# Holding back the early conversions of the last weight: a set begin, spacing, and another place in the sync queue

## The chip, the cores and the metric

The kernel runs on one core of one Trainium2 chip. The metric is the device time of one execution in microseconds (us), lower is better; the median of three runs of the kernel before is 587.26 us. PE is the matrix engine, DVE the vector engine, ACT the scalar engine, POOL the GpSimd engine, SP the sync engine, on which almost every transfer is issued. Each of them takes its instructions strictly in the order in which the program lists them.

## What is computed

An attention over 2 batches, 8 heads, 768 positions and head size 64, in which each query sees a band of neighbours and 24 block summaries, and then two feed-forward blocks over the 1536 tokens that it gives:

```
scores = [band(q k^T), q (block max of k)^T + log 32];  a = softmax(scores);  x = a [v ; block mean of v]
h = ((x w1) * (x w2)) w3 w_out            # 512 -> 1024 -> 1024 -> 512
h2 = h w_in;  y = (h2 * clip(h2+3,0,6)/6) w_out2     # 512 -> 2048 -> 512
```

The weights arrive as 8-byte floats.

## The kernel before

Products are done in three passes over pairs of high and low parts, so every operand tile has two halves: `slot(s)[:, 0]` the rounded value, `slot(s)[:, 1]` the rest. **A conversion** of one 128x512 weight tile is a load of 512 KB into a buffer `raw` (SP), two ACT operations (`to_f32`: a scaled copy `c<-raw` of the upper word, and a shift of the lower word in place), two DVE operations on `c`, and then in `to_hi_lo` an ACT copy (high part) and a POOL subtraction (low part). The buffers `raw` and `c` are four each and are taken in turn (`take`).

The weight that is used last, `w_out2` (16 tiles), has no place on the chip yet while attention runs. `convert_out` converts each of its tiles ahead of time, puts high and low part back into the `raw` buffer they came from, and `spill` writes them out to a buffer `wo` in memory (512 KB, on SP); `fetch` brings them back later. So one `raw` buffer goes through load, conversion and write-out before the next load may use it.

The program is not written in the order in which it runs. Every step is an entry of a `Graph` (`g.op`) with its engine, an estimated length, a due time, and the buffers that it reads and writes. `schedule` walks a clock of its own through the entries: an entry is ready when those it depends on are done by the estimates, and of the ready entries of an engine the one that is due first is taken. What it leaves is one fixed order per engine; on the chip, semaphores hold each instruction until its data are there, and everything behind it on the same engine waits with it.

The stretch of the change lies between the loop over token blocks and the second feed-forward block. The loop (`ab`, `acc1`; three blocks `j` of eight pairs) gives PE 36 matmuls of 128x512 for a pair; between them stand the attention tiles of the next block: scores (`probabilities`), softmax on DVE, POOL and ACT, and in `attend` the transposes (PE), two copies `pt` out of the banks (ACT and DVE), the product with V (PE) and its write to `arena`. Each pair's result passes ACT as `ta` and `arena<-tg`. Behind the loop, `sums_of_x` and `w_in_group` prepare the operands of the second block; `w_in_group` uses the same `raw` and `c` buffers, in turn behind the sixteen of `convert_out`. The call stands ahead of both and gives all sixteen tiles the same due time:

```
        sums_of_x(due)
        for n in range(NFC2):
            convert_out(due, w2_in[NFC2 + tile_of(n)], ("wo", n))
        w_in_group(due, 0)
```

An entry with a far due time is still taken as soon as its engine has nothing more urgent that is ready.

Of the kernel before, what the change touches and what calls it, by code (L numbers as in the profile page):

```python
# [30 lines left out]
P = 128  # L31
# [18 lines left out]
NFC, NFC2 = DFF // P, DFF2 // P  # L50
# [10 lines left out]
class Graph:  # L61
# [10 lines left out]
        self.ops = []  # L72
        self.writer, self.readers = {}, {}

    def op(self, eng, ns, due, fn, reads=(), writes=(), lock=False):
        i = len(self.ops)
        deps = set()
        for k in reads:
            if k in self.writer:
                deps.add(self.writer[k])  # L80
            self.readers.setdefault(k, []).append(i)
        for k in writes:
            if k in self.writer:
                deps.add(self.writer[k])
            deps.update(self.readers.get(k, ()))
            self.writer[k] = i
            self.readers[k] = []
        deps.discard(i)
        self.ops.append((eng, ns, due, fn, deps, lock or eng == "pool"))
        return i  # L90

    def schedule(self):
        n = len(self.ops)
        left = [len(o[4]) for o in self.ops]
        users = [[] for _ in range(n)]
        for i, o in enumerate(self.ops):
            for d in o[4]:
                users[d].append(i)

        due = [o[2] if o[0] == "pe" else self.LAST for o in self.ops]  # L100
        for i in range(n - 1, -1, -1):
            for u in users[i]:
                e = self.ops[i][0]
                due[i] = min(due[i], due[u] - self.ops[i][1] - self.LAT.get(e, 40))
        ready_at = [0.0] * n
        engines = sorted({o[0] for o in self.ops})
        free = dict.fromkeys(engines, 0.0)
        coming = {e: [] for e in engines}
        ready = {e: [] for e in engines}
        for i, o in enumerate(self.ops):  # L110
            if not left[i]:
                heapq.heappush(coming[o[0]], (0.0, i))
        order = []
        port = 0.0
        while True:
            best = None
            for e in engines:
                while coming[e] and coming[e][0][0] <= free[e]:
                    i = heapq.heappop(coming[e])[1]
                    heapq.heappush(ready[e], (due[i], i))  # L120
                if ready[e]:
                    t = free[e]
                elif coming[e]:
                    t = coming[e][0][0]
                else:
                    continue
                if best is None or t < best[0]:
                    best = (t, e)
            if best is None:
                break  # L130
            t, e = best
            if not ready[e]:
                free[e] = t
                continue
            i = heapq.heappop(ready[e])[1]
            eng, ns = self.ops[i][:2]
            order.append((t, i))
            if self.ops[i][5]:
                t = max(t, port)
                port = t + ns  # L140
            free[e] = t + ns
            for u in users[i]:
                same = self.ops[u][0] == e
                at = t + ns + (0 if same and e == "pe" else 35 if same else self.LAT.get(e, 40))
                ready_at[u] = max(ready_at[u], at)
                left[u] -= 1
                if not left[u]:
                    heapq.heappush(coming[self.ops[u][0]], (ready_at[u], u))
        assert len(order) == n
        return sorted(order)  # L150
# [8 lines left out]
L3N = 1  # L159
DUE_FF = 29.0  # L160
AHEAD, BEHIND = -27.8, -143.7


def build(tc, qd, kw, vw, kt, vt, consts, wp_in, w12_in, w2_in, out):
# [68 lines left out]
        turn[name] += 1  # L233
        return t

    def load(due, out_fn, in_ap, nbytes, writes):
        g.op("sp", max(450, nbytes / 400.0), due, lambda: nc.sync.dma_start(out=out_fn(), in_=in_ap), (), writes)  # L237

    def to_f32(due, src, pieces=1, banks=None, n_raw=N_RAW):

        r, c = take("raw", n_raw), take("c", N_C)
        kr, kc = ("raw", r), ("c", c)
# [5 lines left out]
        for i in range(pieces):  # L248
            e = slice(i * ne, (i + 1) * ne)
            kri, kci = (kr, kc) if pieces == 1 else ((kr, i), (kc, i))  # L250
            ra = raws[r][:, e]
            load(due - 6 * us, lambda ra=ra: ra, src[:, e], P * ne * 8, [kri] + [kr] * (i == 0))
            w = ra.bitcast(U32).rearrange("p (n two) -> p n two", two=2)
            wf = ra.bitcast(F32).rearrange("p (n two) -> p n two", two=2)
            hw, lw = w[:, :, 1], w[:, :, 0]
# [50 lines left out]

    def spill(due, key, src_fn, reads):
        d = spilled[key]
        g.op("sp", 1300, due, lambda: nc.sync.dma_start(out=d, in_=src_fn()), reads, [key])

    def fetch(due, s, key):
        d = spilled[key]
        g.op("sp", 1300, due, lambda: nc.sync.dma_start(out=slot(s).bitcast(F32), in_=d), [key], both(s))

    def convert_out(due, src, key, lo="pool"):

        r, c, parts = to_f32(due, src)
        e, f, cf, keys = parts[0]
        w = raws[r].bitcast(F32R).rearrange("p (two n) -> p two n", two=2)
        kr = [("raw", r)]  # L320
        to_hi_lo(due, 1, lambda: cf, keys, lambda: w[:, 0, :], lambda: w[:, 1, :], kr, kr, lo)
        spill(due, key, lambda: raws[r].bitcast(F32).rearrange("p (two n) -> p two n", two=2), kr)
# [355 lines left out]
    with tc.manual_schedule():  # L678
# [169 lines left out]

        sums_of_x(due)
        for n in range(NFC2):  # L850
            convert_out(due, w2_in[NFC2 + tile_of(n)], ("wo", n))
        w_in_group(due, 0)
        w_in_group(due, 1)
        prev = []
# [168 lines left out]
```

## Time and profile before

| | before |
|---|---|
| median of 3 runs (lowest to highest) | 587.26 us (587.2 to 587.62) |
| the profiled execution, its own time | 587.12 us |
| its span in the trace | 585.1 us |
| PE busy, share of the span | 541.2 us, 92% |
| DVE, ACT, POOL busy | 345.5, 283.0, 217.5 us |
| mean granted clock of PE | 0.985 |

PE is busy for 92% of the span; the span is 2.02 us shorter than the execution's own time. Clock values are shares of PE's full clock (1.00 is 2.4 GHz, 0.5 is 1.2 GHz); a mean between them is a mixture of the two over a stretch.

### The profile page before, as it was taken

Reading aid. Unit: us, or ns where it says so; the run is one execution under the profiler, and the core shown is the slowest. Engines: PE = TensorE matmul, PEld = TensorE weight load, DVE = VectorE, ACT = ScalarE, POOL = GpSimd, SP = SyncE. Lnnn points to the kernel's source line nnn. Section 1 sums busy time; section 2 is a strip of 40 time slices with the busy share of each in tenths; the row PEclk is TensorE's granted clock in tenths of the full one; section 3 lists DMA queues with packets and bytes.
Section 4 is the critical chain, followed back from the end, with each engine's and each line's share of the span. In section 5 each row is a group of like instructions: output and inputs, shape, how many; then the busy total and the mean of one; then the engine's idle time right before and its main releaser. Section 6 shows DMA issues by size and latency. Waiting matters only on the chain.

```text
span 585.1 us, 8146 instructions
## 1 busy us (share of the span) xinstructions
PE 541.2 (92%) x3032; PEld 441.3 (75%) x3032; DVE 345.5 (59%) x464; ACT 283.0 (48%) x483; POOL 217.5 (37%) x178
## 2 busy tenths in 40 slices
PE   0679999999999939969999999999999999999997
PEld 0457788887778728758888888888888888888885
DVE  5899978877895737477853487888545222221000
ACT  2788877437445434434444487675544422222001
POOL 0578656894443324329134374555300000000000
PEclk9999999999999978979999999999999999999999
DMA  8999873756437664627354547733489921001521
GB/s 307 375 349 333 233 251 109 216 176 211 150 113 242 203 234 115 229 73 289 107 206 181 185 169 259 272 153 147 154 310 366 399 93 56 0 1 73 188 100 72
DMA packets 42111, 112.62 MB, mean 192 GB/s; under 512 B 4040, under 2 KB 13512, under 8 KB 42072
## 3 DMA queue, kind: packets, MB, share of 16 engines
q1 hardware_dynamic: 41928, 111.97, 56.0%
q8 instruction: 24, 0.39, 0.3%
q10 hardware_dynamic: 144, 0.13, 0.1%
q14 instruction: 15, 0.12, 0.1%
HBM read 82.17 MB, written 28.31 MB: 189 GB/s over the span
## 4 chain that ended last, share of the span: by engine, by line
PE 76%; DMA 11%; DVE 4%; POOL 3%; ACT 2%; issue 2%; SPq 1%; POOLq 0%; ACTq 0%; DVEq 0%
PE bank L338 72%; DMA wo<-raw 5%; DMA raw<-in_w_dram 4%; PE bank L522 2%; DMA kres<-in_kt_dram 1%; DMA qst<-in_q_dram 1%; PE bank L507 1%; PE bank L460 1%; POOL arena L295 1%; DVE st L491 1%; DVE c L283 1%; POOL raw L295 1%; POOL sc L497 1%; SPq L237 1%; ACT sc L488 1%
## 5 line engine op out<-in xcount | busy, mean ns | idle before, releaser
L338 PE MATMUL bank<-arena 128*128 128x512 f32 x1152 | 278.3, 395 | 1.1 <-DVE arena L673 0.7
L338 PEld LDWEIGHTS bank<-arena 128*128 128x128 f32 x1152 | 215.6, 189 | 48.5 <-issue 1.4
L338 PE MATMUL bank<-arena,w 128*128 128x512 f32 x816 | 197.1, 392 | 0.0
L338 PEld LDWEIGHTS bank<-arena,w 128*128 128x128 f32 x816 | 153.3, 189 | 32.4 <-issue 0.3
L557 DVE TENSOR_TENSOR arena<-tg,arena 128x512 fp32r<-128x512 f32 x68 | 59.2, 873 | 31.5 <-ACT arena L552 30.3
L552 ACT ACTIVATE arena<-tg 128x512 fp32r<-128x512 f32 x72 | 44.9, 627 | 33.1 <-DVE tg L576 16.9
L264 ACT ACTIVATE c<-raw 128x512 f32<-128x512 f32 x48 | 31.9, 666 | 53.1 <-DMA raw<-in_w_dram 45.3
L279 DVE SCALAR_TENSOR_TENSOR c<-c,raw 128x512 uint32<-128x512 uint32 x48 | 46.5, 979 | 18.2 <-ACT raw L270 17.4
L295 POOL TENSOR_TENSOR arena<-c,arena 128x512 fp32r<-128x512 f32 (+1 forms) x34 | 42.4, 1260 | 32.5 <-ACT arena L292 32.5
L338 PE MATMUL bank<-late,arena 128*128 128x512 f32 x192 | 46.6, 389 | 0.0
L270 ACT ACTIVATE raw<-raw 128x512 uint32<-128x512 uint32 (+1 forms) x72 | 46.5, 655 | 0.0
L283 DVE SCALAR_TENSOR_TENSOR c<-raw,c 128x512 uint32<-128x512 uint32 x48 | 44.5, 943 | 0.1
L295 POOL TENSOR_TENSOR w<-c,w 128x512 fp32r<-128x512 f32 x24 | 34.2, 1428 | 25.9 <-ACT w L292 25.9
L338 PEld LDWEIGHTS bank<-late,arena 128*128 128x128 f32 x192 | 36.0, 188 | 7.5
L612 DVE SCALAR_TENSOR_TENSOR tg<-ta,bank 128x512 f32<-128x512 f32 x16 | 11.0, 689 | 50.2 <-ACT ta L608 50.2
L295 POOL TENSOR_TENSOR raw<-c,raw 128x512 fp32r<-128x512 f32 x16 | 23.3, 1472 | 37.6 <-ACT raw L292 33.8
L608 ACT ACTIVATE ta<-bank,three 128x512 f32<-128x512 f32 x16 | 11.0, 687 | 48.9 <-PE bank L338 48.9
L576 DVE TENSOR_TENSOR tg<-ta,bank 128x512 f32<-128x512 f32 x24 | 16.3, 679 | 26.6 <-PE bank L338 25.6
L497 POOL TENSOR_TENSOR sc<-sc,st 128x960 f32<-128x960 f32 x12 | 22.2, 1850 | 23.1 <-DVE st L493 22.1
L636 DVE TENSOR_SCALAR c<-bank 128x256 f32<-128x256 f32 x1 | 0.4, 423 | 49.3 <-ACT c L634 49.3
L522 PE MATMUL bank<-pt,vall 120*64 120x64 f32 x384 | 15.5, 240 | 14.5 <-ACT pt L514 14.5
L487 POOL TENSOR_TENSOR sc<-sc,st 128x960 f32<-128x960 f32 x12 | 23.0, 1919 | 15.5 <-DVE st L485 15.5
(61 smaller groups left out, 501.1 us busy)
## 6 DMA issues: line engine op xcount, KB each, us to landing
raw<-in_w_dram SPq DMA_DIRECT2D x48, 512.0 KB, 4.0
raw<-in_wp_dram SPq DMA_DIRECT2D x22, 512.0 KB, 7.7
wo<-raw SPq DMA_DIRECT2D x16, 512.0 KB, 5.0
wi<-w SPq DMA_DIRECT2D x16, 512.0 KB, 2.6
gj<-arena SPq DMA_DIRECT2D x16, 512.0 KB, 3.4
w<-wi SPq DMA_DIRECT2D x16, 512.0 KB, 5.7
arena<-gj SPq DMA_DIRECT2D x16, 512.0 KB, 3.3
arena<-wo SPq DMA_DIRECT2D x12, 512.0 KB, 4.3
```

The lines of the kernel that those rows point to most:

```text
L264: lambda uf=uf, wf=wf: nc.scalar.activation(out=uf, in_=wf[:, :, 1], func=AF.Copy, scale=2.0**-112),
L270: lambda lw=lw: nc.scalar.activation(out=lw, in_=lw, func=AF.Copy, scale=2.0**-29 * (1 - eps), bias=7.5 * eps - 0.5),
L279: lambda ui=ui, lw=lw: nc.vector.scalar_tensor_tensor(out=ui, in0=ui, scalar=3, in1=lw, op0=ALU.logical_shift_left, op1=ALU.bitwise_or),
L283: lambda ci=ci, ui=ui, hw=hw: nc.vector.scalar_tensor_tensor(out=ci, in0=hw, scalar=0x80000000, in1=ui, op0=ALU.bitwise_and, op1=ALU.bitwi ...
L295: lambda: e.tensor_tensor(out=lo(), in0=src(), in1=hi().bitcast(F32), op=ALU.subtract),
L338: nc.tensor.matmul(out=out_ap, lhsT=lhs(a), rhs=rhs(c), start=start and n == 0, stop=stop and n == 3 * len(terms) - 1, skip_group_check=skip,)
L487: lambda: nc.gpsimd.tensor_tensor(out=s8, in0=s8, in1=wide(0), op=ALU.subtract), [("st", i2)], skeys)
L497: lambda: nc.gpsimd.tensor_tensor(out=s8, in0=s8, in1=wide(1), op=ALU.mult), [("st", i2)], skeys)
L522: nc.tensor.matmul(out=bank[b0][h * D : (h + 1) * D, p * P + x * QT : p * P + (x + 1) * QT], lhsT=vall[vi[x]][0:NK, (2 * p + h) * D : (2 * ...
L552: g.op("act", 630, due, lambda: nc.scalar.activation(out=slot(s)[:, 0, :], in_=src_ap, func=AF.Copy), [src_key], [("t", s, 0)])
L557: lambda: eng.tensor_tensor(out=slot(s)[:, 1, :], in0=src_ap, in1=slot(s)[:, 0, :].bitcast(F32), op=ALU.subtract), [src_key, ("t", s, 0)], ...
L576: g.op("dve", 685, due, lambda: nc.vector.tensor_tensor(out=gf, in0=a, in1=bank[5], op=ALU.mult), [("bank", 5), ("ta", n % 2)], [("tg", n ...
```

## The change

`Graph.op` takes two more numbers. `begin` is the earliest time, on the scheduler's own clock, at which the entry counts as ready. `slack` is added to the time at which its users count as ready. `convert_out` gives its load of tile n a begin of 180 + 6.5 n us and a slack of 6 us, and the write-out to `wo` a slack of 3 us, so that a later load into the same buffer and the fetch count as ready later. No instruction is added or removed and no buffer changes; only the orders change.

```
-        ready_at = [0.0] * n
+        ready_at = [float(o[7]) for o in self.ops]
...
-                heapq.heappush(coming[o[0]], (0.0, i))
+                heapq.heappush(coming[o[0]], (ready_at[i], i))
...
-                ready_at[u] = max(ready_at[u], at)
+                ready_at[u] = max(ready_at[u], at + self.ops[u][6])
...
+HOLD = 6000.0
+OUT_AT, OUT_STEP = 180, 6.5
...
-            load(due - 6 * us, lambda ra=ra: ra, src[:, e], P * ne * 8, [kri] + [kr] * (i == 0))
+            load(due - 6 * us, lambda ra=ra: ra, src[:, e], P * ne * 8, [kri] + [kr] * (i == 0), slack, begin)
...
-        g.op("sp", 1300, due, lambda: nc.sync.dma_start(out=d, in_=src_fn()), reads, [key])
+        g.op("sp", 1300, due, lambda: nc.sync.dma_start(out=d, in_=src_fn()), reads, [key], slack=HOLD / 2)
...
-        r, c, parts = to_f32(due, src)
+        r, c, parts = to_f32(due, src, slack=HOLD, begin=begin)
...
-            convert_out(due, w2_in[NFC2 + tile_of(n)], ("wo", n))
+            convert_out(due, w2_in[NFC2 + tile_of(n)], ("wo", n), begin=(OUT_AT + OUT_STEP * n) * us)
```

What that does to the orders is seen at three places. The names are those of the program with the number of each tile: raw_112 to raw_115 and c_116 to c_119 are the four buffers of each kind, wo_63 to wo_78 the sixteen write-outs; line numbers of the kernel after are higher by two or three in the rows shown.

On ACT, ahead of the copy `pt_154<-bank_131` of the third block's first attention tile, before the change:

```order
L264 ACTIVATE c_119<-raw_112 128x512
L270 ACTIVATE raw_112<-raw_112 128x512
L264 ACTIVATE c_118<-raw_115 128x512
L292 ACTIVATE raw_113<-c_116 128x512
L574 ACTIVATE ta_120<-bank_129 128x512
L270 ACTIVATE raw_115<-raw_115 128x512
L264 ACTIVATE c_117<-raw_114 128x512
L514 ACTIVATE pt_154<-bank_131 120x512
L488 ACTIVATE sc_153<-sc_153 128x960
```

and after it:

```order
L267 ACTIVATE c_118<-raw_115 128x512
L273 ACTIVATE raw_115<-raw_115 128x512
L295 ACTIVATE raw_115<-c_118 128x512
L577 ACTIVATE ta_120<-bank_129 128x512
L267 ACTIVATE c_119<-raw_112 128x512
L555 ACTIVATE arena<-tg_122 128x512
L517 ACTIVATE pt_154<-bank_131 120x512
L491 ACTIVATE sc_153<-sc_153 128x960
```

Before, three conversions start in these nine rows (`c_119`, `c_118`, `c_117`), the last right ahead of the copy, and thirteen of the sixteen tiles have their first step ahead of the copy. After, one conversion start (`c_119<-raw_112`) stands between the result `ta` of the pair and the copy, and it is the fourth of the sixteen.

On PE, the same place, from the transposes (`con,sc`) to the first rows of the product with V (`pt,vall`), before:

```order
L507 MATMUL bank_132<-con,sc_152 120x128 x4
L507 MATMUL bank_131<-con,sc_152 120x128 x4
L338 MATMUL bank_125<-arena 128x512 x3
L338 MATMUL bank_126<-arena 128x512 x3
L338 MATMUL bank_127<-arena 128x512 x3
L338 MATMUL bank_128<-arena 128x512 x3
L522 MATMUL bank_131<-pt_154,vall_146 64x64 x2
L522 MATMUL bank_131<-pt_155,vall_147 64x64 x2
```

and after:

```order
L510 MATMUL bank_132<-con,sc_152 120x128 x4
L510 MATMUL bank_131<-con,sc_152 120x128 x4
L341 MATMUL bank_125<-arena 128x512 x3
L341 MATMUL bank_126<-arena 128x512 x3
L525 MATMUL bank_131<-pt_154,vall_146 64x64 x2
L525 MATMUL bank_131<-pt_155,vall_147 64x64 x2
```

The product with V has moved up past two of the four groups of three matmuls that stood between.

On SP, the middle of the write-outs before the change, up to the loads for the last attention tile:

```order
L309 DMA wo_67<-raw_113 128x1024
L237 DMA raw_113<-in_w_dram 128x512
L309 DMA wo_70<-raw_112 128x1024
L237 DMA raw_112<-in_w_dram 128x512
L309 DMA wo_69<-raw_115 128x1024
L237 DMA raw_115<-in_w_dram 128x512
L309 DMA wo_72<-raw_114 128x1024
L237 DMA kall_145<-in_kw_dram 128x4x160
L237 DMA qst_151<-in_q_dram 128x512
```

and after it, from the first load of the sixteen:

```order
L239 DMA raw_113<-in_w_dram 128x512
L239 DMA raw_114<-in_w_dram 128x512
L312 DMA wo_63<-raw_113 128x1024
L239 DMA raw_115<-in_w_dram 128x512
L312 DMA wo_64<-raw_114 128x1024
L239 DMA kall_145<-in_kw_dram 128x4x160
L239 DMA qst_151<-in_q_dram 128x512
L239 DMA raw_112<-in_w_dram 128x512
L312 DMA wo_65<-raw_115 128x1024
L239 DMA raw_113<-in_w_dram 128x512
```

Before, nine of the sixteen write-outs stand ahead of `kall_145` and `qst_151`, each with a load of the next tile behind it; after, two do. The first load stood 17 rows further up in the old order and now stands behind the K, Q and V loads that came after it there. Writes and loads still alternate.

## Rows read from the trace of the kernel before

**Rows 1.** Waits of PE: us in total, times, longest us.
```profile
PE bank L522 <- ACT pt L514: 14.5, 3, 10.0
```

**Rows 2.** PE by time: start, us, line, operation; [idle before, releaser].
```profile
146.99 1.52 PE L338 MATMUL bank<-arena 128*128 128x512 f32 x6
...
162.59 1.12 PE L507 MATMUL bank<-con,sc 128*120 128x128 f32 x8 [0.58 <-DVE sc L471]
...
168.40 29.76 PE L338 MATMUL bank<-arena 128*128 128x512 f32 x130 [0.17 <-DVE arena L539]
198.09 1.05 PE L460 MATMUL bank<-kall,qst 64*64 64x120 f32 x32
...
205.07 1.13 PE L507 MATMUL bank<-con,sc 128*120 128x128 f32 x8 [0.22 <-DVE sc L471]
205.95 2.98 PE L338 MATMUL bank<-arena 128*128 128x512 f32 x12
218.88 1.98 PE L522 MATMUL bank<-pt,vall 120*64 120x64 f32 x32 [9.95 <-ACT pt L514]
220.79 6.83 PE L338 MATMUL bank<-arena,w 128*128 128x512 f32 x24
...
254.83 1.98 PE L522 MATMUL bank<-pt,vall 120*64 120x64 f32 x32 [3.86 <-ACT pt L514]
256.74 2.93 PE L338 MATMUL bank<-arena 128*128 128x512 f32 x6
259.46 1.64 PE L507 MATMUL bank<-con,sc 128*120 128x128 f32 x8
261.79 1.15 PE L522 MATMUL bank<-pt,vall 120*64 120x64 f32 x32 [0.69 <-ACT pt L514]
```

**Rows 3.** PE in order of time, after the last attention product.
```profile
295.65 5.60 PE L338 MATMUL bank<-arena,w 128*128 128x512 f32 x24
```

**Rows 4.** Windows: busy us per engine, PEclk the granted clock, DMA share, GB/s.
```profile
218.90:227.50 8.60, 8.60 (x56) 7.01 (x56) 5.21 (x9) 4.71 (x8) 1.79 (x1) 0.75 0.39 109
...
254.80:261.10 6.30, 6.27 (x46) 5.23 (x46) 4.67 (x7) 1.11 (x2) 1.79 (x1) 0.53 0.22 78
```

**Rows 5.** ACT in order of time, ahead of the long wait.
```profile
212.25 0.66 ACT L264 ACTIVATE c<-raw 128x512 f32<-128x512 f32 x1 [4.72 <-DMA raw<-in_w_dram]
...
217.68 0.66 ACT L264 ACTIVATE c<-raw 128x512 f32<-128x512 f32 x1 [3.21 <-DMA raw<-in_w_dram]
218.25 0.58 ACT L514 ACTIVATE pt<-bank 120x512 f32<-120x512 f32 x1
```

**Rows 6.** The chain that ended last, 190 to 262 us: start, us, what.
```profile
190.60 5.16 DMA raw<-in_w_dram
...
208.32 5.11 DMA wo<-raw
...
213.48 4.12 DMA raw<-in_w_dram
```

**Rows 7.** The waits of the SP queue, from 160 to 280 us.
```profile
SPq L237 <- DMA wo<-raw: 49.0, 16, 7.7
```

**Rows 8.** Line 309, issues of write-outs: ns min/median/max, first and last start.
```profile
L309 SPq DMA_DIRECT2D wo<-raw x16: 319/338/423, 171.0 to 273.3; - x16
```

**Rows 9.** The chain of the whole execution, its last long piece.
```profile
262.94 318.49 PE bank L338 x1404
```

**Rows 10.** The page, part 6: loads of weight tiles, us to landing.
```profile
raw<-in_w_dram SPq DMA_DIRECT2D x48, 512.0 KB, 4.0
```

**Rows 11.** SP in order of time: one issue of a K window.
```profile
208.75 0.57 SPq L237 DMA_DIRECT2D kall<-in_kw_dram  x1
```

**Rows 12.** DVE in order of time: one conversion step alone and one beside POOL.
```profile
160.46 1.42 DVE L279 SCALAR_TENSOR_TENSOR c<-c,raw 128x512 uint32<-128x512 uint32 x1
...
178.70 0.69 DVE L279 SCALAR_TENSOR_TENSOR c<-c,raw 128x512 uint32<-128x512 uint32 x1 [1.71 <-ACT raw L270]
```

**Rows 13.** POOL in order of time, the same stretch.
```profile
159.54 1.79 POOL L497 TENSOR_TENSOR sc<-sc,st 128x960 f32<-128x960 f32 x1 [4.15 <-DVE st L493]
```

More of the change, by code (lines that the diff above doesn't have):

```diff
@@ L73, in __init__, with op @@
         self.writer, self.readers = {}, {}
-    def op(self, eng, ns, due, fn, reads=(), writes=(), lock=False):
+    def op(self, eng, ns, due, fn, reads=(), writes=(), lock=False, slack=0, begin=0):
         i = len(self.ops)
@@ L88, in op @@
         deps.discard(i)
-        self.ops.append((eng, ns, due, fn, deps, lock or eng == "pool"))
+        self.ops.append((eng, ns, due, fn, deps, lock or eng == "pool", slack, begin))
         return i
@@ L234, in take, with load, to_f32 @@
         return t
-    def load(due, out_fn, in_ap, nbytes, writes):
-        g.op("sp", max(450, nbytes / 400.0), due, lambda: nc.sync.dma_start(out=out_fn(), in_=in_ap), (), writes)
-    def to_f32(due, src, pieces=1, banks=None, n_raw=N_RAW):
+    def load(due, out_fn, in_ap, nbytes, writes, slack=0, begin=0):
+        g.op("sp", max(450, nbytes / 400.0), due, lambda: nc.sync.dma_start(out=out_fn(), in_=in_ap), (), writes,
+             slack=slack, begin=begin)
+    def to_f32(due, src, pieces=1, banks=None, n_raw=N_RAW, slack=0, begin=0):
         r, c = take("raw", n_raw), take("c", N_C)
@@ L313, in fetch, with convert_out @@
         g.op("sp", 1300, due, lambda: nc.sync.dma_start(out=slot(s).bitcast(F32), in_=d), [key], both(s))
-    def convert_out(due, src, key, lo="pool"):
-        r, c, parts = to_f32(due, src)
+    def convert_out(due, src, key, lo="pool", begin=0):
+        r, c, parts = to_f32(due, src, slack=HOLD, begin=begin)
         e, f, cf, keys = parts[0]
```

## The prediction

> **What bounds the kernel now.** I read the page first: PE is busy for 92% of the span, so time is to be had where PE stands still or runs slowly. The waits of PE name the place: 14.5 us in three waits for ACT's copy `pt` (line 514), one of them 10.0 us [rows 1]. PE in order of time shows where [rows 2]. From 198.09 us on, the waits are 0.22 us (at 205.07), 9.95 (at 218.88), 3.86 (at 254.83) and 0.69 (at 261.79); all but the first are the product with V (line 522) waiting for `pt`. Ahead of them stand 0.58 us (at 162.59) and 0.17 us (at 168.40). Behind 262.94 us the chain of the whole execution is one piece of PE work of 318.49 us [rows 9]: nothing that other engines do there holds PE up.
>
> Why is `pt` late? ACT in order of time gives the long wait [rows 5]: the copy at 218.25 stands behind two conversion starts (line 264), at 212.25 and 217.68, and ACT was idle for 4.72 and 3.21 us ahead of them, waiting for a load of the last weight. The copy needs no such load; it only stands behind it. The chain through this stretch continues to the load (4.12 us from 213.48) and to a write-out `wo` of 5.11 us from 208.32 [rows 6]: the load could not be issued before its buffer had been written out. SP waited 49.0 us in all for such write-outs between 160 and 280 us [rows 7]. So a ring of four buffers, at its own speed, sets when ACT gets on, and PE's attention tiles hang on ACT.
>
> The windows show a second cost [rows 4]: behind the waits the granted clock is 0.75 on the mean (218.9 to 227.5 us) and 0.53 (254.8 to 261.1), a mixture of the levels 1.2 and 2.4 GHz, though PE is busy throughout.
>
> **The change part by part.** No instruction is added, so nothing is paid for as such; the question is which waits go.
>
> *ACT's order.* Ahead of the first late copy thirteen conversion starts become four, and of its pair only one stays. Taken away: 9.95 + 3.86 + 0.69 us for `pt` [rows 2]. The 0.22, 0.58 and 0.17 us are waits for DVE's scores and write to `arena`; at 160.46 a conversion step (line 279) of 1.42 us stands directly ahead of that work on DVE [rows 12], and now none does in that stretch. Sum of waits: 15.47 us.
>
> *PE's clock.* The work that ran slowly was: a product with V of 1.98 us against 1.15 (at 261.79), twice, 1.66 us; 24 matmuls in 6.83 us (at 220.79) against 5.60 [rows 3], 1.23 us; six in 2.93 us (at 256.74) against 1.52 (at 146.99), 1.41 us; eight transposes in 1.64 us (at 259.46) against 1.13 (at 205.07), 0.51 us [rows 2]. Sum 4.81 us. The fall follows each long wait, so it goes with it.
>
> Together 20.28 us; against the profiled execution's own 587.12 us that leaves 566.84. The median of the three runs is 587.26, so 0.14 us either way.
>
> *What is late next.* The sixteen conversions now fall into the stretch from about 180 us to the second feed-forward block, and two things can be late. I follow the new orders by the old durations. First, the copy that was late by 9.95 us. Without waits the scores of line 460 run at 198.09, the transposes end at about 205.7 (205.95 less the 0.22), and after half of the 12 matmuls behind them (1.4 us) the product could start at about 207.1; in the new order two of the four groups stand ahead of it. On SP `kall_145` waits until those scores have read its old content, 199.07; it and `qst_151` take some 0.6 us each to issue [rows 11], so `raw_112` is issued at about 200.3 and landed at 204.3 by the page's median of 4.0 us [rows 10]. ACT then does the conversion start (0.66 us), one split of a pair (about as long) and the copy (0.58): 206.2, or 0.9 us before it is needed. A slow load of 5.16 us, as the load from 190.60 in the same chain took [rows 6], would still be in time on paper, but each of the four steps between adds its semaphore. Lower end of this term 0; upper end, taken from the shortest of the old waits for `pt`, 0.69 us [rows 2], for each of the four tiles, 2.8 us. I take 0.7, one such wait, since for the other three copies the loads are issued about a pair of PE work ahead.
>
> Second, the last attention tile's result goes straight into the first pair of the third block, and x of the second block is written on the same ACT and DVE at that time; before, PE waited there for nothing. I put 0.3 us on it (bounds 0 and the 0.58 us that DVE cost at 162.59). So 566.84 + 0.7 + 0.3 = **567.8 us**.
>
> *Behind attention.* Six conversions and the first four of `w_in_group` then remain, and their loads stand on SP behind fetches of `wo` into places that PE frees only pair by pair. From the last attention tile to the first product with `w_705` PE has eight pairs of 36 matmuls, 67 us at 5.60/24 us each [rows 3]. At the average pace of the sixteen write-outs, 171.0 to 273.3 us [rows 8], 6.4 us each, ten conversions need 64 us, so this just fits at the old pace, and that pace held the very waits for the ring that ACT had. Its single steps are far shorter: a load of 4.0 us, a write-out of 5.1 [rows 6, 10] and six steps between of 0.7 us each, one of them on POOL longer, some 5 us [rows 5, 12], give 14 us for a buffer, and four buffers go round, 3.5 us each, 35 us for ten. I take this as hidden; uncovered, it is the third rival.
>
> The GPSIMD Engine Reference of the Trainium skill (Specifications) speaks against the change: GpSimd shares its memory interfaces with VectorE, and VectorE instructions with two on-chip inputs contend with it. The trace agrees on one pair: the step at 160.46 took 1.42 us beside POOL's 1.79 us from 159.54, and the same step at 178.70 took 0.69 us alone [rows 12, 13]. That gives a rival of its own.
>
> **The rivals.**
> 1. *The same wait, shorter* (0.14). If a load lands behind the copy's time by more than the 0.9 us, PE waits once as at 254.83: 3.86 us and the slow clock behind it, 0.83 + 1.41 + 0.51 = 2.75 us; 567.8 + 6.6 = 574.4. For it: writes and loads still alternate on SP, and `kall_145` now waits there for PE. Against: four conversions ahead, not thirteen.
> 2. *DVE and POOL collide* (0.12). The two DVE steps of a conversion now share their stretch with the two softmax passes of POOL on each of four tiles. If each tile's product is late by one collision, 1.42 - 0.69 = 0.73 us, that is 2.9 us less the 0.7 already in: 570.0. Against: DVE is busy for 5.21 of 8.60 us from 218.9 us on [rows 4], so most steps find it free early.
> 3. *The second block starts late* (0.05): slower. Were the ring held to one conversion per pair of PE work, 8.4 us (36 matmuls at 5.60/24), ten would need 84 us where there are 67: 17 us of wait at the first product with `w_705`, and slow clock behind it of the 2.75 us above. It goes on from there: each later group needs two conversions, 16.8 us, beside 66 matmuls, 15.4 us, so six more groups add 8.4 us. 567.8 + 17 + 2.8 + 8.4 = 596. It decides once a conversion takes more than some 8.4 us; between 6.7 and that it eats part of the gain. For it: the fetches on SP; against: the 3.5 us that the buffers allow.
> 4. *Nothing gained* (0.03): if PE's stretch from 198 us on is bound by something that stands behind the late loads, as the softmax, the wait stays: 587. Against: the copy itself ended the wait, and the row ahead of it was the conversion [rows 2, 5].
>
> **How the numbers follow.** My forecast has 0.66: 567.8 us, by itself 566 (the sum without residue, less 0.8 for the small waits between kinds of matmul that may go too) to 570.2 (both residues at their upper ends). Rivals 1 and 2 reach to 574.4. Leaving out 3 and 4 (0.08) and tails, the range is 565.5 to 574.5. A change is told from none beyond about 0.2% (1.2 us) here. Faster by more: 0.66 + 0.14 + 0.12 = 0.92; within it: 0.03 (rival 4); slower: 0.05 (rival 3).
>
> **What the profile would show.** Right: no wait of line 522's successor for `pt` above 1 us; granted clock 1.00 from 195 us to the end; the first write-out behind 180 us instead of at 171.0; SP's wait for write-outs below 49.0 us; PE in one piece from about 242 us on. Wrong in size: waits of 0.7 to 4 us at the four products with V, with line 264's successor ahead of `pt` on ACT (rival 1) or a stretched DVE step (rival 2). Wrong altogether: an idle PE at its first product with `w_705`, some 67 us behind the loop's last attention tile (rival 3), or the 10 us wait where it was. What would make it wrong most easily is a load on SP that stands behind a write-out which itself waits for ACT.

## The result, and the profile after

| | before | after |
|---|---|---|
| median (lowest to highest) | 587.23 us (586.02 to 587.62, 4 runs) | 571.68 us (571.13 to 572.83, 4 runs) |
| span of the profiled execution | 585.1 us | 570.9 us (its own time 572.83 us) |
| PE busy | 541.2 us, 92% | 537.8 us, 94% |

The ratio of the two is 0.9741, with a 95% interval of 0.972 to 0.9762: faster by 15.55 us. The forecast was 567.8 us in a range of 565.5 to 574.5, faster by 19.4 us. So the direction and the range held, and 3.9 us of the forecast gain are not there. The profiled execution is the slowest of the four, 1.15 us above the median, so what is read from it below has to account for some more. On another chip the same two kernels gave 585.78 and 570.35 us (ratio 0.9738, 0.9718 to 0.9758, the run `after_again` below): the gain is the same, the level is not.

In the kernel after, every line number of `build` stands two or three higher: the product with V is L525 (was 522), its copy `pt` L517 (514), the conversion start L267 (264), the write-out L312 (309), the fetch L316 (313), the feed-forward matmuls L341 (338), `ta` L577 (574).

The waits of PE over the whole span, of after (engine and line that waited, what for; us in total, times, longest):

```profile
PE bank L341 <- ACT ta L577: 2.0, 1, 2.0
...
PE bank L525 <- ACT pt L517: 0.7, 1, 0.7
PE bank L341 <- DVE arena L676: 0.7, 1, 0.7
PE bank L341 <- ACT arena L538: 0.7, 1, 0.7
PE bank L341 <- ACT late_f L826: 0.6, 1, 0.6
```

The 14.5 us for `pt` [rows 1] are down to 0.7. The window over the stretch in which they stood (columns: us of the window, then busy us and count of PE, PEld, DVE, ACT, POOL, then PEclk, DMA share, GB/s) shows PE busy throughout at a granted clock of 1.00, where single windows had 0.75 and 0.53 before [rows 4]:

```profile
198.00:262.00 64.00, 63.94 (x482) 51.39 (x482) 49.78 (x62) 33.36 (x58) 32.62 (x21) 1.00 0.59 196
```

PE in order of time, after, at the places that the argument comes back to (start, us, ..., in brackets the idle time ahead and who ended it):

```profile
163.96 1.67 PE L341 MATMUL bank<-arena 128*128 128x512 f32 x6
165.47 1.03 PE L510 MATMUL bank<-con,sc 128*120 128x128 f32 x8
167.24 1.15 PE L525 MATMUL bank<-pt,vall 120*64 120x64 f32 x32 [0.74 <-ACT pt L517]
169.09 3.28 PE L341 MATMUL bank<-arena 128*128 128x512 f32 x12 [0.70 <-ACT arena L538]
...
199.50 1.05 PE L463 MATMUL bank<-kall,qst 64*64 64x120 f32 x32
...
277.69 5.60 PE L341 MATMUL bank<-arena,w 128*128 128x512 f32 x24
...
312.70 3.01 PE L341 MATMUL bank<-arena,w 128*128 128x512 f32 x12 [2.04 <-ACT ta L577]
...
321.72 1.65 PE L341 MATMUL bank<-arena,w 128*128 128x512 f32 x6 [0.57 <-ACT late_f L826]
```

**The balance.** Two points of PE's work can be found in every execution: the scores that ran at 198.09 us [rows 2], and the group of 24 matmuls that ran at 295.65 [rows 3]. They cut the span in three: ahead of the first, between the two, and behind the second. "+" is longer than before.

| | scores | the 24 matmuls | span | ahead | between | behind |
|---|---|---|---|---|---|---|
| before | 198.09 | 295.65 | 585.1 | 198.09 | 97.56 | 289.45 |
| after | 199.50 | 277.69 | 570.9 | +1.41 | -19.37 | +3.76 |
| after, on the other chip | 198.68 | 276.52 | 568.4 | +0.59 | -19.72 | +2.43 |

The row of before is of the first chip, and the third row is set against it too. The 289.45 us behind hardly depend on the chip: they are 289.39 to 289.47 us in the executions below in which PE waits for nothing there.

The stretch between gave all that the waits and the clock there were counted at. What is missing was lost at both sides of it.

**The place behind.** The chain that ended last, of after, runs through this stretch not on PE alone, as before [rows 9], but through the ring (start, us, what):

```profile
284.88 12.03 PE bank L341 x53
296.91 0.40 SPq L316
297.31 0.05 issue
297.36 7.03 DMA wo<-raw
304.39 0.02 issue
304.40 4.30 DMA raw<-in_w_dram
```

ACT in order of time, after, shows what hung on that load:

```profile
308.79 1.21 ACT L267 ACTIVATE c<-raw 128x512 f32<-128x512 f32 x2 [3.46 <-DMA raw<-in_w_dram]
309.90 1.19 ACT L273 ACTIVATE raw<-raw 128x512 uint32<-128x512 uint32 x2
311.00 0.61 ACT L295 ACTIVATE w<-late_f 128x512 fp32r<-128x512 f32 x1
311.52 0.65 ACT L267 ACTIVATE c<-raw 128x512 f32<-128x512 f32 x1
312.08 0.57 ACT L577 ACTIVATE ta<-bank 128x512 f32<-128x512 f32 x1
```

Read the two together: SP issued a fetch at 296.91 us and only behind it the write-out; that took 7.03 us; the load into the same buffer 4.30 us more; ACT idled 3.46 us for it; and the copy `ta`, which needs no load, stood behind it on ACT and let PE idle 2.04 us. It is the mechanism of the wait that was removed [rows 5, 6], in a new place and smaller. The program's order names the parties: the write-out is that of the last of the sixteen tiles, the load behind it is already one for `w_in`, and PE's 2.04 us stand ahead of the first product of the second block, which is to write the bank that `ta` has yet to read. The fetch had stood on SP since 295.79 us and was released by PE only at 296.91; how much of the wait that delay makes, no run here takes apart.

### The profile page after: what moved, and what is told of

The parts are those of the page before. It is cut to its first block, busy times and chain, and to the rows that moved or that the text cites. A ratio compares the mean times of both kernels' runs of the same rounds, so it can differ in the third digit from the quotient of the medians.

```text
span 570.9 us, 8140 instructions
## 1 busy us (share of the span) xinstructions
PE 537.8 (94%) x3032; PEld 437.3 (77%) x3032; DVE 344.8 (60%) x464; ACT 281.9 (49%) x483; POOL 216.1 (38%) x178
## 4 chain that ended last, share of the span: by engine, by line
PE 83%; DMA 6%; DVE 4%; POOL 3%; ACT 2%; issue 2%; SPq 1%; ACTq 0%; DVEq 0%; POOLq 0%
PE bank L341 77%; PE bank L525 2%; DMA raw<-in_w_dram 2%; PE bank L463 2%; PE bank L510 1%; DMA kres<-in_kt_dram 1%; DMA qst<-in_q_dram 1%; POOL arena L298 1%; DMA wo<-raw 1%; DVE c L286 1%; POOL sc L500 1%; ACT c L267 0%; SPq L239 0%; DVE bank L282 0%; DVE sc L474 0%
## 5 line engine op out<-in xcount | busy, mean ns | idle before, releaser
L341 PE MATMUL bank<-arena 128*128 128x512 f32 x1152 | 278.2, 394 | 2.5 <-POOL arena L298 1.1
L341 PEld LDWEIGHTS bank<-arena 128*128 128x128 f32 x1152 | 214.6, 189 | 50.4 <-POOL arena L298 2.3
L341 PE MATMUL bank<-arena,w 128*128 128x512 f32 x816 | 196.6, 391 | 2.7 <-ACT ta L577 2.0
L341 PEld LDWEIGHTS bank<-arena,w 128*128 128x128 f32 x816 | 152.3, 188 | 36.2 <-ACT ta L577 2.9
L560 DVE TENSOR_TENSOR arena<-tg,arena 128x512 fp32r<-128x512 f32 x68 | 56.1, 825 | 26.3 <-ACT arena L555 25.5
L282 DVE SCALAR_TENSOR_TENSOR c<-c,raw 128x512 uint32<-128x512 uint32 x48 | 45.0, 944 | 16.7 <-ACT raw L273 16.4
L267 ACT ACTIVATE c<-raw 128x512 f32<-128x512 f32 x48 | 31.7, 665 | 33.2 <-DMA raw<-in_w_dram 27.2
L286 DVE SCALAR_TENSOR_TENSOR c<-raw,c 128x512 uint32<-128x512 uint32 x48 | 47.8, 1011 | 0.2
L341 PE MATMUL bank<-late,arena 128*128 128x512 f32 x192 | 46.6, 389 | 0.0
L298 POOL TENSOR_TENSOR raw<-c,raw 128x512 fp32r<-128x512 f32 x16 | 22.0, 1380 | 56.4 <-ACT raw L295 55.0
L341 PEld LDWEIGHTS bank<-late,arena 128*128 128x128 f32 x192 | 36.0, 188 | 7.5
L298 POOL TENSOR_TENSOR w<-c,w 128x512 fp32r<-128x512 f32 x24 | 35.7, 1491 | 11.7 <-ACT w L295 11.3
L490 POOL TENSOR_TENSOR sc<-sc,st 128x960 f32<-128x960 f32 x12 | 22.3, 1856 | 22.1 <-DVE st L488 22.1
L577 ACT ACTIVATE ta<-bank 128x512 f32<-128x512 f32 x24 | 14.2, 591 | 33.2 <-PE bank L341 33.0
L637 ACT ACTIVATE c<-bank 128x512 f32<-128x512 f32 (+1 forms) x12 | 6.8, 578 | 45.4 <-PE bank L341 45.2
```

What stands on the lines that cost most here:

```text
L267: lambda uf=uf, wf=wf: nc.scalar.activation(out=uf, in_=wf[:, :, 1], func=AF.Copy, scale=2.0**-112),
L282: lambda ui=ui, lw=lw: nc.vector.scalar_tensor_tensor(out=ui, in0=ui, scalar=3, in1=lw, op0=ALU.logical_shift_left, op1=ALU.bitwise_or),
L286: lambda ci=ci, ui=ui, hw=hw: nc.vector.scalar_tensor_tensor(out=ci, in0=hw, scalar=0x80000000, in1=ui, op0=ALU.bitwise_and, op1=ALU.bitwi ...
L298: lambda: e.tensor_tensor(out=lo(), in0=src(), in1=hi().bitcast(F32), op=ALU.subtract),
L341: nc.tensor.matmul(out=out_ap, lhsT=lhs(a), rhs=rhs(c), start=start and n == 0, stop=stop and n == 3 * len(terms) - 1, skip_group_check=skip,)
L490: lambda: nc.gpsimd.tensor_tensor(out=s8, in0=s8, in1=wide(0), op=ALU.subtract), [("st", i2)], skeys)
```

## The experiments

Two theories of the gain and three of the remainder were at hand. **A**: the begins carry the gain, because ACT's copies no longer stand behind conversions whose loads are absent; against it, that the new place of the loads on SP does. **B**: the remainder behind 277 us is ACT standing behind starts whose buffer is still being written out; against it **C**, the second block's own load on ACT and POOL, and **D** and **E**, that any other order pays elsewhere. Times of before are those of the same chip.

**1. The begins alone.**

```
-HOLD = 6000.0
+HOLD = 0.0
```

> The kernel after with both slacks at 0 and the begins kept. Theory A (the begins carry the gain: the late copies no longer stand on ACT behind conversions whose loads are absent; the slacks only reorder the sync queue): 571.7 us within 2, no wait for pt above 1 us between 200 and 262 us. Rival (the place of the loads in the sync queue carries a good part): 577 to 586 us, with a wait for pt of several us.

Measured: 571.78 us (before 586.54; ratio 0.9762, 0.9734 to 0.9791). As by A: the ratio of the whole change within its interval, and no wait for `pt` behind 200 us. The slacks are not needed. The begins move the loads on SP too, as the orders ahead of the prediction show, so this run tells the begins from the slacks, but not ACT's order from SP's; run 5 leaves both orders as they were. The profiled execution here is the slowest of its five (574.73 us), and its part behind the 24 matmuls is 5.79 us longer than before.

**2. The slacks alone.**

```
-OUT_AT, OUT_STEP = 180, 6.5
+OUT_AT, OUT_STEP = 0, 0.0
```

> The kernel after with the begins at 0 and both slacks kept. Theory A: conversions stand between the late copies as in the kernel before, so the ring of four buffers holds the copies again: 583 to 589 us, PE waits for pt of 7 to 14 us in sum behind 200 us. Rival (the sync queue's order carries the gain): 570 to 576 us, no such wait.

Measured: 572.74 us (ratio 0.9776, 0.9751 to 0.9801). **Theory A missed by more than 10 us**: the begins aren't needed either. The two parts overlap; each alone gives almost all.

What a slack does must be put right here. The line `ready_at[u] = max(ready_at[u], at + self.ops[u][6])` adds the slack of the entry `u` that is to become ready, not of the one that it waits for. So it is the load itself that counts as ready 6 us later, behind the write-out that frees its buffer, and the write-out itself that counts as ready 3 us later, behind the last step on its tile. The fetch is not held back. Every write-out passes through `spill`, so those of later weights and products get the 3 us too.

PE in order of time, slacks alone, shows what they cost in place of the long wait:

```profile
165.80 1.13 PE L510 MATMUL bank<-con,sc 128*120 128x128 f32 x8 [1.40 <-DVE sc L474]
167.67 1.15 PE L525 MATMUL bank<-pt,vall 120*64 120x64 f32 x32 [0.74 <-ACT pt L517]
169.52 0.73 PE L341 MATMUL bank<-arena 128*128 128x512 f32 x2 [0.70 <-ACT arena L538]
171.93 29.73 PE L341 MATMUL bank<-arena 128*128 128x512 f32 x130 [1.68 <-DVE arena L542]
```

Here four conversions have started by 158.52 us again (before: by 155.65), and DVE holds PE for 1.40 and 1.68 us. Directly ahead of the second wait two conversion steps stand on DVE (2.88 us from 168.40); ahead of the first stand none, so that one is not shown to be theirs. The scores run at 201.59 us (+3.50), the 24 matmuls at 281.03 (between: -18.12), and the 289.47 us behind are those of before.

**3 and 4. Each slack by itself.** What the slacks do must be in the orders: counted there, the starts of conversions of `w_out2` ahead of the first late `pt` on ACT are 13 before, 4 after, 10 with both slacks or that on the load, 12 with that on the write-out. Theory A2: the copy is late if the ring has not got through the starts ahead of it.

```
-OUT_AT, OUT_STEP = 180, 6.5
+OUT_AT, OUT_STEP = 0, 0.0
...
-        g.op("sp", 1300, due, lambda: nc.sync.dma_start(out=d, in_=src_fn()), reads, [key], slack=HOLD / 2)
+        g.op("sp", 1300, due, lambda: nc.sync.dma_start(out=d, in_=src_fn()), reads, [key], slack=0)
```

and, for the write-out's slack alone, in place of the last two lines:

```
-        r, c, parts = to_f32(due, src, slack=HOLD, begin=begin)
+        r, c, parts = to_f32(due, src, slack=0, begin=begin)
```

> Begins at 0, the slack of 6 us on the load kept, that on the write-out at 0. Of the sixteen conversions of w_out2, 10 then start on ACT ahead of the first late copy pt, as with both slacks; 13 do in the kernel before, 4 in the kernel after. Theory A2 (what counts is only how many starts stand ahead of a copy, against the pace of the ring; 10 are done by then, 13 are not): 571 to 575 us, no wait for pt over 1.5 us behind 200 us. Rival (the write-outs' place in the sync queue does it): 578 to 586 us.

> Begins at 0, the slack of 3 us on the write-out kept, that on the load at 0. 12 conversions of w_out2 start on ACT ahead of the first late copy. Theory A2: one conversion less than before, so the copy waits 9.95 us less one step of the ring (3.5 us by a quarter of a buffer's round, 6.4 us by the write-outs' average pace), that is 3.5 to 6.5 us, with slow clock behind it: 576 to 583 us. Rival: 571 to 575 us, no such wait.

Measured: 574.5 us (ratio 0.9802, 0.9787 to 0.9818) with the load's slack, and 586.37 us (before 585.89; 1.0006, 0.9993 to 1.002) with the write-out's. The first is as A2 said: even before, the tenth start ran at 200.65 us, ahead of the transposes at 205.07 [rows 2], and the thirteenth only at 217.68 [rows 5]. The second missed its 576 to 583 us. PE in order of time, with the write-out's slack alone:

```profile
216.74 1.97 PE L525 MATMUL bank<-pt,vall 120*64 120x64 f32 x32 [6.59 <-ACT pt L517]
...
255.06 1.97 PE L525 MATMUL bank<-pt,vall 120*64 120x64 f32 x32 [3.90 <-ACT pt L517]
```

The wait is 3.36 us shorter [rows 2], of which 1.22 us only because PE comes to it later: the product runs 218.88 - 216.74 = 2.14 us sooner. One start fewer brought the copy forward by 2.14 us, less than the 3.5 to 6.4 us that I had put on a step of the ring. The step was not the error: before, it took 217.68 - 212.25 = 5.43 us [rows 5]. But the ring itself ran later in this order, for the twelfth start came 3.30 us later than before. ACT in order of time, with the write-out's slack alone:

```profile
215.55 0.66 ACT L267 ACTIVATE c<-raw 128x512 f32<-128x512 f32 x1 [6.33 <-DMA raw<-in_w_dram]
```

Even the 2.14 us were not kept: in this order six of the matmuls that stood ahead of the product stand behind it, at the slow clock (2.93 us at 218.65 us, against 1.52 [rows 2]), and the later product, with as many starts ahead of its copy as before, runs at 255.06 us as it did at 254.83 [rows 2].

**5. The write-outs cut to a quarter, order of before.** If the ring holds the copy, a ring with the same order and shorter write-outs must let it go.

```
+        m = TB // 4 if key[0] == "wo" else TB
...
-        g.op("sp", 1300, due, lambda: nc.sync.dma_start(out=d, in_=src_fn()), reads, [key])
+        g.op("sp", 1300, due, lambda: nc.sync.dma_start(out=d[:, :, 0:m], in_=src_fn()[:, :, 0:m]), reads, [key])
```

The fetch reads `d[:, :, 0:m]` four times over in the same way.

> The kernel before with only a quarter of each write-out of w_out2 (128 of 512 columns of each half; the fetch repeats the quarter), so the products with w_out2 are of other numbers, in the same time. Same order everywhere. Theory A (the ring's write-outs hold ACT, and ACT the copy): each write-out lands some 2 to 3.5 us sooner; three laps lie ahead of the first late copy, so its wait of 9.95 us falls to 0 to 4 us, and the later ones of 3.9 and 0.7 us below 2: 571 to 580 us. Rival (the copy is late by ACT's, DVE's or POOL's own work on conversions, not by the write-outs): 584 to 588 us, the 10 us wait in place.

Measured: 573.66 us (ratio 0.9792, 0.9776 to 0.9809). PE in order of time, at the first late copy (its lines stand two higher than before):

```profile
211.32 1.15 PE L524 MATMUL bank<-pt,vall 120*64 120x64 f32 x32 [3.24 <-ACT pt L516]
212.41 5.74 PE L340 MATMUL bank<-arena,w 128*128 128x512 f32 x24
```

No instruction moved on any engine, and most of the gain is there: the 9.95 us are 3.24, and the work behind runs at full clock (1.00 from 211.3 to 218.0 us). So the length of the ring's write-outs makes 6.71 us of the wait; that is shown, not argued. What makes the 3.24 us that are left is not taken apart. The quarter makes the other transfers lighter too: between 160 and 230 us the median from issue to landing fell from 5.1 to 3.7 us for a write-out, by 1.4 us where I had expected 2 to 3.5, and from 4.4 to 4.1 us for a load.

**6. The same cut in the kernel after.** The lines are those of 5.

> The kernel after with only a quarter of each write-out of w_out2 (128 of 512 columns of each half; the fetch repeats the quarter), so the products with w_out2 are of other numbers, in the same time. Theory B (what is left at 302 to 322 us is ACT standing behind a start whose buffer is still being written out): the waits of 2.04 and 0.57 us shrink below 0.7 in sum, 568 to 570 us. Rival C (ACT's and POOL's own load at the start of the second block): 571 to 572.5 us, the waits in place.

Measured: 568.16 us (before 585.78; ratio 0.9703, 0.9679 to 0.9728), against 570.35 us for the kernel after on the same chip. On this chip the kernel after waits less in that place than in its first execution, 0.70 and 0.53 us instead of 2.04 and 0.57. PE in order of time, kernel after, this chip:

```profile
301.86 5.76 PE L341 MATMUL bank<-arena,w 128*128 128x512 f32 x24 [0.70 <-ACT ta L577]
...
319.28 7.46 PE L341 MATMUL bank<-arena,w 128*128 128x512 f32 x30 [0.53 <-ACT late_f L826]
```

The same with the quarter, from 276.96 us on (its lines stand two higher than after):

```profile
276.96 5.60 PE L343 MATMUL bank<-arena,w 128*128 128x512 f32 x24
...
301.44 5.60 PE L343 MATMUL bank<-arena,w 128*128 128x512 f32 x24
306.88 2.88 PE L343 MATMUL bank<-arena 128*128 128x512 f32 x12
309.60 2.88 PE L343 MATMUL bank<-arena,w 128*128 128x512 f32 x12
312.32 2.88 PE L343 MATMUL bank<-arena 128*128 128x512 f32 x12
315.04 9.68 PE L343 MATMUL bank<-arena,w 128*128 128x512 f32 x42
```

Theory B: no wait is left there, and the part behind is 566.4 - 276.96 = 289.44 us, as before, where the kernel after has 291.88 us on this chip. ACT's and POOL's own work was the same, so C falls. Ahead of it a wait of 0.65 us for `ta` stands at 257.79 us, which the kernel after does not have.

**7. The first groups of `w_in` ahead in the ring.** B asks whether their place in the ring is at fault.

```
         for n in range(NFC2):
+            if n == 12:
+                w_in_group(due, 0)
+                w_in_group(due, 1)
             convert_out(due, w2_in[NFC2 + tile_of(n)], ("wo", n), begin=(OUT_AT + OUT_STEP * n) * us)
-        w_in_group(due, 0)
-        w_in_group(due, 1)
```

> The kernel after, with the first two groups of w_in put into the ring ahead of the last four conversions of w_out2 instead of behind all sixteen. Theory B (what the change left on the table at 302 to 322 us is ACT standing behind starts of conversions whose buffer is still being written out, so the copy ta and late_f of the second block are late by 2.0 + 0.6 us and some idle time ahead of them): these two waits go, 568.5 to 570 us. Rival C (PE would wait there for the first groups of w_in anyhow, by ACT's or POOL's own load): 571 to 572.5 us with the waits in place. Rival D (the last four write-outs are late for their fetches): over 572.5 us, with a new wait on arena<-wo later.

Measured: 574.18 us (before 586.54; ratio 0.9814, 0.9786 to 0.9842), within rival D's bounds, but not by its mechanism: PE waits for no fetch. ACT in order of time, and PE, in this kernel:

```profile
313.61 0.67 ACT L267 ACTIVATE c<-raw 128x512 f32<-128x512 f32 x1 [4.84 <-DMA raw<-in_w_dram]
...
319.28 0.66 ACT L267 ACTIVATE c<-raw 128x512 f32<-128x512 f32 x1 [2.48 <-DMA raw<-in_w_dram]
...
321.35 0.60 ACT L826 ACTIVATE late_f<-bank 128x512 f32<-128x512 f32 x1
```

```profile
322.00 9.83 PE L341 MATMUL bank<-arena,w 128*128 128x512 f32 x36 [4.15 <-ACT late_f L826]
```

By the program's order all sixteen starts for `w_out2` are done by 304 us here. The starts at 313.61 and 319.28 us are those of the third group of `w_in`, whose loads go into buffers that the last conversions of `w_out2` still have to write out: the chain that ended last runs through POOL's low part to 309.74 us, a write-out of 5.09 us and a load of 4.31 us to the start at 319.28. The copy `late_f` stands behind it on ACT, and PE idles 4.15 us. So it is not whose conversions come last, but that the starts stand ahead of a copy on ACT before their loads can land.

**8. Begins closer together.**

```
-OUT_AT, OUT_STEP = 180, 6.5
+OUT_AT, OUT_STEP = 180, 5.0
```

> The kernel after with the begins 5.0 us apart instead of 6.5: the last conversion begins 22.5 us earlier on the planner's clock. Theory B (the loss at 302 to 322 us is a matter of the conversions being late in the ring): that loss shrinks, 569 to 571.5 us, as long as the late copies pt stay clear. Rival E (the ring is at its own speed between 200 and 300 us, so closer begins only put conversions ahead of pt again): waits for pt of 1 to 6 us come back, 573 to 578 us.

Measured: 575.87 us (ratio 0.9826, 0.9802 to 0.985): rival E. Five starts instead of four stand ahead of the first late copy, which is late by 1.42 us; and the copies `ta` and `late_f` further on are still late (0.61, 0.70 and 1.60 us between 288 and 325 us). Theory B's loss did not shrink: the part behind the 24 matmuls, which run at 279.40 us, is 573.8 - 279.40 = 294.40 us, 4.95 us longer than before, and that is the larger share of what this run loses.

**9 to 11. Both slacks with one begin for all tiles**, at 180 and at 185 us, and the kernel after beside them on one chip.

```
-OUT_AT, OUT_STEP = 180, 6.5
+OUT_AT, OUT_STEP = 180, 0.0
```

> Both slacks kept, all begins at 180 us without spacing. Theory F (with the slacks the planner's own ring paces the conversions; the begin only has to keep them out of 160 to 172 us, where the kernel with the slacks alone loses 1.4 + 1.7 us to DVE): 568 to 571 us, no wait at 160 to 172 us beyond the 0.74 + 0.70 us that stand there in the kernel after, and less idle time at 300 to 325 us than there. Rival E (closer starts cost at pt and at late_f as with begins 5.0 us apart): 573 to 577 us.

> The kernel after, unchanged, on the chip of the three runs beside it: 570.5 to 573 us by both theories.

> Once more both slacks with all begins at 180 us, beside the kernel after on one chip. Theory F: 1.5 to 3 us below it (568.5 to 571 us). Rival (569.55 was a matter of that chip): within 1.2 us of it.

> Both slacks, all begins at 185 us: 4 conversions of w_out2 stand on ACT ahead of the first late copy, as in the kernel after; 5 with 180 us, where that copy was late by 0.92 us. Theory A2 (the count ahead of the copy sets its wait): that wait goes, 568 to 570 us. Rival E (what is pushed back is missed at 300 to 325 us): waits for ta or late_f there again, 570 to 573 us.

Measured with 180 us: 569.55 us (before 585.89; ratio 0.9724, 0.9707 to 0.9741), and on the next chip 570.08 us against 570.35 us for the kernel after (0.9732, 0.9713 to 0.9752, against 0.9738). On one chip the two can't be told apart: 0.27 us, where theory F had 1.5 to 3 us, so its rival was right on the time. Of F's mechanism half held: the losses behind are gone (568.0 - 278.60 = 289.40 us), but the first late copy, with five starts ahead, is late by 0.77 to 0.92 us, and 0.70 us stand at 248 us. With 185 us: 577.41 us (ratio 0.9857, 0.9837 to 0.9876). Four starts ahead of the copy, no wait there, as A2 said; but the total was missed by 7 us, by rival E's way and more. PE in this kernel, with 24 matmuls that take 5.60 us [rows 3] taking 8.51:

```profile
308.00 8.51 PE L341 MATMUL bank<-arena,w 128*128 128x512 f32 x24 [3.74 <-ACT ta L577]
```

ACT, in the same kernel, just ahead of it:

```profile
305.19 1.21 ACT L267 ACTIVATE c<-raw 128x512 f32<-128x512 f32 x2 [4.28 <-DMA raw<-in_w_dram]
306.30 0.64 ACT L273 ACTIVATE raw<-raw 128x512 uint32<-128x512 uint32 x1
306.84 0.62 ACT L295 ACTIVATE w<-late_f 128x512 fp32r<-128x512 f32 x1
307.36 0.58 ACT L577 ACTIVATE ta<-bank 128x512 f32<-128x512 f32 x1
```

No version here beats the kernel after by what a measurement can tell, save that with a quarter of the write-outs, which leaves work out.

## Why the prediction was right, and what it mis-sized

**What bounds the kernel: right.** The copy stood behind starts that stood behind the ring: shorter write-outs with every order as it was (5) cut the wait from 9.95 to 3.24 us, and an order with nine starts fewer ahead of the copy (1) removes it.

**The terms between the two points: right.** 20.28 us were counted, 0.75 of them ahead of 198 us; 19.53 us remain for the stretch between, and 19.37 and, on the other chip, 19.72 us were measured. The slow clock went with the waits (1.00 throughout).

**The two residues: too high.** For 0.7 us at the first late copy and 0.3 us at the third block's first pair nothing was paid: neither place waits. This 1.0 us too much covered a part of what follows, by luck.

**The 0.58 and 0.17 us ahead of 198 us: wrong in what takes their place.** "Now none does" was right of DVE, and these two waits went. But 0.74 and 0.70 us stand at the next product and behind it. Before, six matmuls stood between that tile's transposes and its product; in the new order they stand ahead of the transposes (the rows at 163.96 to 167.24 above), and nothing covers the copies. I had read the new order on ACT, DVE and SP at this tile, not on PE. The exchange costs 0.69 us, and with the 0.75 us that I had counted as gain the step is off by 1.44 us. The whole difference ahead is +1.41 in one execution, +0.59 in another and +0.08 us in that of run 6, with the same order there and the same two waits. What goes beyond the 0.69 us differs from one execution to the next, in both directions, and can't be put down to the change.

**"Behind attention ... I take this as hidden": the term that was mis-sized.** It was set at 0 and costs 2.43 us (on the chip of run 6, which shows it to be the ring) to 3.76 us (in the first execution); the two waits named above are 1.23 and 2.61 us of that, and the rest is not broken down. Three things in the step were off. Sixteen write-outs from 171.0 to 273.3 us have fifteen steps between them, 6.8 us each and not 6.4, so at that pace ten conversions need 68 us where there are 67, which does not fit, and by the third rival's own bound of 6.7 us a part of the gain was at stake. The ring does not go round at 3.5 us a conversion: in the kernel after, ten steps of starts from 260.19 to 311.52 us take 5.1 us each, and from 177.40 us on before, nine steps up to 222.59 us take 5.0 us each. By that pace ten conversions do fit into the 67 us; but the deadline was not only when the operands of the second block's first product are there. It is every copy that stands behind a start on ACT, pair by pair, and the one at 312.08 us came too late, so that this product waited for its bank. The signs named for this, "an idle PE at its first product" of the second block, and a load on SP behind a write-out that waits itself, are what the rows show; I had given them to a rival of 17 us and asked only whether it comes to that. In the first execution the sum then closes: 566.84 us, and 2.16 ahead (1.41, and the 0.75 counted as gain), 0.16 between and 3.76 behind, are 572.92, with 572.83 us measured.

**The rivals.** 1, the same wait shorter, did not happen in the kernel after, and is what 5 and 8 show: 3.24 and 1.42 us. 2, DVE and POOL: the collision is there and is covered. DVE's conversion step, in order of time, and POOL's softmax pass beside it, of after:

```profile
211.22 2.01 DVE L282 SCALAR_TENSOR_TENSOR c<-c,raw 128x512 uint32<-128x512 uint32 x1
...
213.87 0.69 DVE L282 SCALAR_TENSOR_TENSOR c<-c,raw 128x512 uint32<-128x512 uint32 x1
```

```profile
210.89 1.79 POOL L500 TENSOR_TENSOR sc<-sc,st 128x960 f32<-128x960 f32 x1 [4.62 <-DVE st L496]
```

The step took 2.01 us beside POOL and 0.69 us alone, and PE waited for neither. The sharing that the Trainium skill states (GPSIMD Engine Reference, Specifications) is seen in these rows, and cost nothing here. 3, the second block late: its mechanism, at 2.4 to 3.8 us of its 17. 4, nothing gained, because something behind the late loads binds PE: it fell with the wait. The run at 586.37 us (write-out's slack alone) gains nothing either, but there `pt` is still what PE waits for.

**The signs.** The first write-out stands at 190.8 us instead of 171.0 [rows 8], SP waits 21.9 us for write-outs instead of 49.0 [rows 7] from 160 to 280 us (33.4 up to 340 us, since the ring now goes on longer; before, it is 49.0 up to there as well), the clock is 1.00 from 195 us, and no `pt` waits over 1 us: right. PE in one piece from 242 us on: wrong, by the 2.04 and 0.57 us.

**Open.** Why the slack on the load suffices at the block's later tiles too is not told apart. Counting the first starts for `w_in`, 14 stand ahead of the second tile's copy, as before, and 17 instead of 18 ahead of the third's, which was late by 3.86 us before and is not late there. The ring got to its eighteenth start at 243 us there and at 252 us before, and loads, copies and scores wait for one another on both ACT and SP.

## What to carry to other kernels

When a slow ring of buffers feeds an engine that also serves the critical path, count at each critical instruction how many ring steps the program order puts ahead of it, and compare that with the ring's measured pace; the planner's clock decided here: holding each load back 6 us behind the write-out that frees its buffer was worth nearly as much as a hand-set begin. A ring that is moved out of one stretch meets the next: ask of every instruction behind its steps, not only of the data's last user, when it is due. And read the new order on the waiting engine too: a cover that stood between two dependent steps may have moved.

## What the runs showed of the hardware

TensorE's granted clock fell behind some waits and not behind others. Behind idle times of 9.95, 6.59, 3.90 and 3.86 us the product with V took 1.97 to 1.98 us (before, from 218.88 to 220.86 us, at a clock of 0.50, that is 1.2 GHz); behind one of 3.24 us (run 5) it took 1.15 us, and the 24 matmuls behind it 5.74 us, at 1.00. So in that run a wait that was only shortened gave back its slow clock as well: 9.95 us became 3.24, and the run was 12.2 us faster.

The length of a wait alone does not settle it. With both slacks (2) and with the load's alone (3), PE stands idle for the same four short times in a row between 164 and 173 us: 1.40, 0.74, 0.70 and 1.68 us. Behind them, from 172 to 176 us, the clock was 1.00 in the first execution and 0.57 in the second, and 130 matmuls took 29.73 and 31.36 us. PE in order of time, the load's slack alone (the row to set beside it, at 171.93 us, stands under run 2):

```profile
172.12 31.36 PE L341 MATMUL bank<-arena 128*128 128x512 f32 x130 [1.68 <-DVE arena L542]
```
